# Attention start reordered: two pulls on two queues, score pairs one step later, post-mix weights loaded first

## The chip, the cores and the metric

The kernel runs on one core of one Trainium2 chip. The metric is the time of one launch on the device in microseconds (us). The engines named below are PE (TensorE, matmuls), ACT (ScalarE), DVE (VectorE), POOL (GpSimd) and SP, which computes nothing here and issues DMAs; ACT can issue DMAs too.

## The reference

Attention over 2 batches, 12 heads, 448 rows and head size 64, in which the heads are mixed by a 12x12 matrix before the softmax and by another one after it, and then two gated layers on 896 tokens of width 768 with a hidden width of 2048.

```python
scores = scale * np.matmul(q, k.transpose(0, 1, 3, 2))
scores = np.einsum('bhij,hg->bgij', scores, w_pre)
scores = scores - np.max(scores, axis=-1, keepdims=True)
attn = np.exp(scores)
attn = attn / (np.sum(attn, axis=-1, keepdims=True) + 1e-09)
attn = np.einsum('bhij,hg->bgij', attn, w_post)
out = np.matmul(attn, v)
...
h = x @ w_in
g = h * np.clip(h + 3.0, 0.0, 6.0) / 6.0
x = g @ w_out
...
h = x @ w_in
g = np.maximum(h, 0.0) + alpha * np.minimum(h, 0.0)
out = g @ w_out
```

## The kernel before

The attention rows are cut into 8 tiles, four for each batch: three of 120 rows and one of 88. A tile has 12 heads, and its scores are made as 6 pairs of heads (`qk`, L205: 8 matmul records on PE for a pair). The two score arrays of a pair lie in PSUM until they are copied to the tile's array `S` in SBUF: one by ACT, the other by DVE. The pairs take turns in two PSUM tags: in the prelude `mx` and `sc` alternate, and from step 0 on only `sc` is used, which has two buffers, room for one pair.

The mix over heads needs heads and rows on the partitions together. So `S` is rearranged by SBUF-to-SBUF DMAs, the pulls (`pull`, L221): each brings one group of up to 10 rows times 12 heads, 120 partitions, into one half of a `pull` buffer. There are 90 groups and four buffers of two groups.

The program then goes through steps p = -2 to 45 in an order written out by hand (the loop over `p_`); there is no other scheduler, and each engine runs its own instructions in that order. Step p works on groups 2p and 2p+1:

- pulls for step p+3 are issued by SP (all six for steps 0 to 2 in step -2), then the loads of v, k and q listed for this step (`load_at`, `load_q_at`);
- `premix` (L234) mixes the two groups into two PSUM buffers of tag `mx`; where a score pair is due at this step, its matmuls are emitted in between (`emit`), ACT copies one of its arrays ahead of the exponentials and DVE the other behind its maxima;
- DVE takes the row maxima (L242), ACT the exponentials (`exp`, L251), DVE the reciprocal of the sum, and POOL scales the post-mix weights `wpost` by it (`wr`, L263);
- `post` (L274) does the post-mix of step p-1, ACT copies it to `MT` (L289; one half goes to DVE once the score pairs are over), and `av` (L341, L320) multiplies finished tiles by v on some steps.

The table `qk_at` says at which step each pair of tiles 1 to 7 is made. Before the change, tile 1's six pairs stand at steps -2 and -1, three each, and the pairs of tiles 2 to 7 at steps 0 to 35, one each. Tile 0's pairs come ahead of everything. `load_q_at` follows from this table: the q of a tile is loaded 3 steps ahead of its first pair, 6 for tile 4. The k of the second batch comes in six loads, at steps 7 to 12. The first weights of the gated layers are loaded inside the same loop (`load_w`, L399, `wst`): the first block in two halves at steps 17 and 18, and ACT takes its magnitude (`conv_abs`, L411) at step 19, ahead of the post-mix copies of that step.

From about 163 us to the end the span holds the gated layers, one long chain of matmuls on PE (L529), which the change doesn't touch.

## Time and profile before

| what | value |
|---|---|
| median of the runs | 645.3 us (641.83, 645.3, 645.5) |
| profiled execution | 640.25 us, its span 638.5 us |
| PE busy | 627.0 us of the span, 98% |
| ACT, DVE, POOL busy | 345.3, 415.9, 294.0 us |
| granted TensorE clock | 0.999 of full |
| DMA | 81.69 MB, mean 128 GB/s |

The profiled execution is one run of the program, timed from outside at 640.25 us; its span, from the first to the last instruction, is what the rows show. Busy shares are means over stages that have different limits, so the stages are looked at one by one. A matmul record's end is modelled, so that a PE which waits between the parts of a mix can look busy; how far the steps lie apart shows such waits.

### The profile page before, as it was taken

The page shows a single profiled execution, that of the slowest core. Times are in us where ns is not written, and L with a number is a line of the kernel's source. Part 1 is how long each engine was busy: PE and PEld are TensorE (multiplying, and loading weights), DVE is VectorE, ACT ScalarE, POOL GpSimd, SP SyncE. Part 2 cuts the span into 40 slices and gives each one's busy share as a digit, 9 for nine tenths or more (in the row PEclk, how much of TensorE's full clock was granted, in tenths as well). Part 3 has the DMA queues.
Part 4 walks back from the last instruction along what each step waited for, and adds up shares of the span by engine and source line. Part 5 has one row for each costly group of instructions (what it writes and reads, how often), then busy time and mean ns, then how long its engine had stood idle before and what let it go on. Part 6 is the DMA issues. An engine that isn't in the chain of part 4 may idle for free.

```text
span 638.5 us, 15698 instructions
## 1 busy us (share of the span) xinstructions
PE 627.0 (98%) x6528; PEld 537.2 (84%) x6528; DVE 415.9 (65%) x653; ACT 345.3 (54%) x632; POOL 294.0 (46%) x241
## 2 busy tenths in 40 slices
PE   7999999999999999999999999999999999999997
PEld 3466667666799999999999999999999999999997
DVE  3765677778666878787545533599999996544301
ACT  4886888987645566655345433444444444444301
POOL 2221123324615454556774645355555556776430
PEclk9999999999999999999999999999999999999999
DMA  7677765756012323333442333123333333445202
GB/s 187 222 197 211 207 188 204 214 177 174 34 50 100 99 100 107 125 115 101 148 148 100 112 136 100 51 100 99 100 102 110 113 113 108 149 159 180 94 1 86
DMA packets 42163, 81.69 MB, mean 128 GB/s; under 512 B 19308, under 2 KB 32364, under 8 KB 42092
## 3 DMA queue, kind: packets, MB, share of 16 engines
q1 hardware_dynamic: 41516, 80.27, 39.5%
q8 instruction: 51, 0.84, 0.5%
q10 hardware_dynamic: 576, 0.41, 0.3%
q14 instruction: 20, 0.16, 0.1%
HBM read 58.65 MB, written 2.75 MB: 96 GB/s over the span
## 4 chain that ended last, share of the span: by engine, by line
PE 86%; POOL 4%; issue 4%; DMA 3%; DVE 1%; ACT 1%; POOLq 0%; SPq 0%; ACTq 0%
PE p L529 64%; PE sc L205 6%; PE pt L274 5%; PE mx L234 5%; PE av L341 4%; POOL wb L442 2%; POOL wlo L455 2%; DMA wst<-in_w_in_dram 2%; PE av L320 1%; DMA pull<-S 1%; ACT e L251 0%; DMA qst<-in_q_dram 0%; ACT wb L411 0%; DVE wb L427 0%; DVE wb L428 0%
## 5 line engine op out<-in xcount | busy, mean ns | idle before, releaser
L455 POOL TENSOR_TENSOR wlo<-wb,whi 128x768 fp32r<-128x768 f32 (+1 forms) x67 | 128.5, 1918 | 122.4 <-ACT whi L447 122.4
L442 POOL TENSOR_TENSOR wb<-wb,wst 128x768 int32<-128x768 int32 x64 | 125.6, 1963 | 81.7 <-DVE wb L435 67.5
L529 PE MATMUL p<-xh,whi 128*128 128x448 f32 x384 | 140.0, 364 | 0.0
L529 PE MATMUL p<-xl,whi 128*128 128x448 f32 x384 | 139.4, 363 | 0.0
L529 PE MATMUL p<-gl,whi 128*128 128x448 f32 x384 | 139.3, 363 | 0.0
L529 PE MATMUL p<-gh,wlo 128*128 128x448 f32 x384 | 138.9, 362 | 0.2 <-POOL wlo L455 0.2
L529 PE MATMUL p<-gh,whi 128*128 128x448 f32 x384 | 138.8, 361 | 0.0
L529 PE MATMUL p<-xh,wlo 128*128 128x448 f32 x384 | 138.3, 360 | 0.0
L427 DVE TENSOR_SCALAR wb<-wb 128x768 f32<-128x768 f32 x64 | 52.6, 822 | 83.4 <-ACT wb L411 83.4
L411 ACT ACTIVATE wb<-wst 128x768 f32<-128x768 f32 x64 | 58.0, 906 | 72.9 <-DMA wst<-in_w_out_dram 51.8
L447 ACT CAST whi<-wb 128x768 fp32r<-128x768 f32 x64 | 53.4, 834 | 47.7 <-PE p L529 29.5
L529 PEld LDWEIGHTS p<-xh,whi 128*128 128x128 f32 x384 | 72.1, 188 | 8.0 <-issue 1.6
L205 PE MATMUL sc<-kst,qst 64*64 64x448 f32 (+2 forms) x384 | 74.7, 575 | 3.7 <-DMA qst<-in_q_dram 3.7
L234 PE MATMUL mx<-pull,wpre 64*64 64x448 f32 (+2 forms) x360 | 74.6, 544 | 2.6 <-ACT e L251 1.7
L529 PEld LDWEIGHTS p<-gh,whi 128*128 128x128 f32 x384 | 72.0, 187 | 5.2
L529 PEld LDWEIGHTS p<-gh,wlo 128*128 128x128 f32 x384 | 71.9, 187 | 5.1 <-POOL wlo L455 0.6
L529 PEld LDWEIGHTS p<-gl,whi 128*128 128x128 f32 x384 | 72.1, 188 | 4.8
L529 PEld LDWEIGHTS p<-xh,wlo 128*128 128x128 f32 x384 | 71.8, 187 | 5.0
L529 PEld LDWEIGHTS p<-xl,whi 128*128 128x128 f32 x384 | 72.1, 188 | 3.9
L242 DVE TENSOR_REDUCE nm<-mx 128x1 f32<-128x448 f32 x90 | 55.1, 622 | 20.2 <-PE sc L205 8.9
L435 DVE SCALAR_TENSOR_TENSOR wb<-wst,wb 128x768 uint32<-128x768 uint32 x64 | 67.5, 1054 | 1.1
L263 POOL TENSOR_SCALAR wr<-wpost,sm 128x60 f32<-128x60 f32 x74 | 24.4, 345 | 93.8 <-DVE sm L259 46.6
(55 smaller groups left out, 772.7 us busy)
## 6 DMA issues: line engine op xcount, KB each, us to landing
wst<-in_w_out_dram SPq DMA_DIRECT2D x32, 768.0 KB
wst<-in_w_in_dram SPq DMA_DIRECT2D x27, 768.0 KB
pull<-S SPq DMA_DIRECT2D x88, 210.0 KB
wst<-in_w_in_dram SPq DMA_DIRECT2D x10, 384.0 KB
out_dram<-o SPq DMA_DIRECT2D x12, 224.0 KB
kst<-in_k_dram SPq DMA_DIRECT2D x11, 224.0 KB
qst<-in_q_dram SPq DMA_DIRECT2D x10, 180.0 KB
v<-in_v_dram SPq DMA_DIRECT2D x4, 168.0 KB
```

Source lines behind the costliest of these rows:

```text
L205: nc.tensor.matmul(ps[o][r:r + z - a, :S], t[D * o:D * o + D, a:z], k_[D * o:D * o + D, j, :], start=True, stop=True,)
L234: nc.tensor.matmul(ms[r][Q * c:Q * c + Q, :S], wpre[a:z], d[a:z, c, :], start=True, stop=True)
L242: nc.vector.tensor_reduce(nm, m[:, :S], axis=AX.X, op=ALU.max, negate=True)
L274: nc.tensor.matmul(ts[c][Q * z:Q * z + Q, u:u + GH], e[a:a + GH, j:j + Q], wr[a:a + GH], start=True, stop=True,)
L341: nc.tensor.matmul(by_half(p[D * o:D * o + D, a % 3, :2 * m]), v_part(T["b"], h, t), MT[ti][:, t:2 * NJ:NJ, h, :m].rearrange("p r (o x) -> ...
L411: nc.scalar.activation(t, s[:, :, 1].bitcast(F32), ACTF.Abs)
L427: nc.vector.tensor_scalar(t, t, W_MAX, W_MIN, ALU.min, ALU.max)
L435: nc.vector.scalar_tensor_tensor(u, st_t[i][:, :, 1], 0xC0000000, u, ALU.bitwise_and, ALU.bitwise_or)
L442: nc.gpsimd.tensor_tensor(n, n, st_t.pop(i)[:, :, 0].bitcast(I32), ALU.add)
L447: nc.scalar.copy(hi, b_t[i])
L455: nc.gpsimd.tensor_tensor(lo[:, a], b_t[i][:, a], w_t[i][0].bitcast(F32)[:, a], ALU.subtract)
L529: nc.tensor.matmul(p, wt[a], xt[c], start=(first and z == 0), stop=(last and z == 2))
```

## The change

Four things are changed. The second pull (group 1) is issued by ACT instead of SP. The loads of the post-mix weights (`wraw`), which stood between the fourth and the fifth pull, go ahead of all pulls, and with them the POOL copy into `wpost`. Of tile 1's six pairs, two each stay at steps -2 and -1, and the last two go to step 0, behind its mix, which is now emitted without a pair in between. All pairs of tiles 2 to 7 come one step later, at steps 1 to 36, and with them the q loads of tiles 3 to 7; the six k loads go to steps 8 to 13.

```diff
--- before.py
+++ after.py
@@ -360,7 +360,7 @@
         qk_at, av_at, av_first = {}, {}, {}
         marked = {NTILE - 1}
         for i in range((NTILE - 1) * (H // 2)):
-            p_ = i // 3 - 2 if i < H // 2 else i - H // 2
+            p_ = i // 2 - 2 if i < 4 else max(i - 5, 0)
             qk_at.setdefault(p_, []).append((1 + i // (H // 2), i % (H // 2)))
         for ti in range(NTILE - 1):
             lo = (tiles[ti]["s"] + tiles[ti]["ng"] - 1) // 2 + 2
@@ -611,6 +611,9 @@
             a = GH * c
             nc.sync.dma_start(out=wpre[Z + GH * c:Z + GH * c + GH, :GH], in_=w_pre[a:a + GH, a:a + GH])
         list(load_q(2))
+        for c in range(2):
+            a = GH * c
+            nc.sync.dma_start(out=wraw[Q * c:Q * c + GH], in_=w_post[a:a + GH, a:a + GH])
         for _ in range(4):
             d_buf.append(late.tile([128, 2, S], F32, tag=f"pull{len(d_buf)}", bufs=1, name="pull"))
             nc.gpsimd.memset(d_buf[-1][:Z], 0.0)
@@ -619,6 +622,9 @@
             v_c.append(late.tile(shape, F32, tag=f"v{c}", bufs=1, name=f"v{c}"))
         seen = late.tile([128, 16], F32, tag="rest", bufs=1, name="rest")[:, :1]
         nc.gpsimd.tensor_scalar(wpre, wpre, scale, 1.0, ALU.mult, ALU.mult)
+        nc.gpsimd.tensor_copy(
+            wpost.rearrange("p (g x) -> p x g", g=H), wraw.rearrange("p (x g) -> p x g", g=H)
+        )
 
         def s_out(pairs):
             for o, (d, s_) in enumerate(pairs):
@@ -673,24 +679,14 @@
                 load_at.setdefault(s_, []).append(lambda b=b, x=x: load_v(b, *x))
 
         for c in range(H // 2):
-            load_at.setdefault(7 + c, []).append(
+            load_at.setdefault(8 + c, []).append(
                 lambda c=c: load_k(1, c % 2, c // 2 * 2, c // 2 * 2 + 2)
             )
 
         for p_ in range(-2, NP + 1):
             if p_ == -2:
                 for g in range(6):
-                    if g == 4:
-                        for c in range(2):
-                            a = GH * c
-                            nc.sync.dma_start(
-                                out=wraw[Q * c:Q * c + GH], in_=w_post[a:a + GH, a:a + GH]
-                            )
-                        nc.gpsimd.tensor_copy(
-                            wpost.rearrange("p (g x) -> p x g", g=H),
-                            wraw.rearrange("p (x g) -> p x g", g=H),
-                        )
-                    pull(g)
+                    pull(g, nc.scalar if g == 1 else nc.sync)
             late_pull = None
             if 0 <= p_ < NP - 3:
                 g = 2 * p_ + 6
@@ -706,7 +702,7 @@
             jobs = qk_at.get(p_, [])
             pair_ = None
             if 0 <= p_ < NP:
-                if jobs:
+                if jobs and p_:
                     emit, pair_ = qk_parts(*jobs[0], "sc")
                     premix(p_, emit)
                     nc.scalar.copy(*pair_[1])
```

On PE, at the first two mixes (the numbers are the program's own count of tiles, and differ between the two programs), this stands before: tile 1's last pair, the mix of step 0 with tile 2's first pair (`qst_121`) in it, and the start of the mix of step 1.

```order
L205 MATMUL sc_234<-kst_91,qst_115 64x448
L205 MATMUL sc_234<-kst_91,qst_115 60x448
L205 MATMUL sc_235<-kst_91,qst_115 64x448
L205 MATMUL sc_235<-kst_91,qst_115 60x448
L234 MATMUL mx_251<-pull_125,wpre_95 64x448 x2
L205 MATMUL sc_250<-kst_91,qst_121 64x448
L205 MATMUL sc_250<-kst_91,qst_121 60x448
L234 MATMUL mx_252<-pull_125,wpre_95 64x448 x2
L205 MATMUL sc_249<-kst_91,qst_121 64x448
L205 MATMUL sc_249<-kst_91,qst_121 60x448
L234 MATMUL mx_282<-pull_127,wpre_95 64x448 x2
```

And now, from the mix of step 0 to the start of the mix of step 1:

```order
L234 MATMUL mx_232<-pull_127,wpre_95 64x448 x2
L234 MATMUL mx_233<-pull_127,wpre_95 64x448 x2
L205 MATMUL sc_247<-kst_91,qst_115 64x448
L205 MATMUL sc_247<-kst_91,qst_115 60x448
L205 MATMUL sc_248<-kst_91,qst_115 64x448
L205 MATMUL sc_248<-kst_91,qst_115 60x448
L205 MATMUL sc_255<-kst_91,qst_115 64x448
L205 MATMUL sc_255<-kst_91,qst_115 60x448
L205 MATMUL sc_256<-kst_91,qst_115 64x448
L205 MATMUL sc_256<-kst_91,qst_115 60x448
L234 MATMUL mx_274<-pull_129,wpre_95 64x448 x2
```

Tile 1's last two pairs (`qst_115`) have moved from ahead of the first mix to between the first and the second.

On ACT, from the copies of tile 1's last pairs (`S_197`) to the exponentials of step 1, before:

```order
L625 COPY S_197<-sc_228 124x448
L625 COPY S_197<-sc_234 124x448
L712 COPY S_248<-sc_250 124x448
L251 ACTIVATE e_267,sm_266<-mx_251,nm_261 128x448
L251 ACTIVATE e_269,sm_266<-mx_252,nm_263 128x448
L712 COPY S_248<-sc_281 124x448
L251 ACTIVATE e_298,sm_297<-mx_282,nm_292 128x448
```

And now, from the last copy of tile 0 (`S_142`) on:

```order
L631 COPY S_142<-sc_183 124x448
L221 DMA pull_127<-S_142 120x1x448
L631 COPY S_197<-sc_198 124x448
L631 COPY S_197<-sc_204 124x448
L631 COPY S_197<-sc_214 124x448
L631 COPY S_197<-sc_220 124x448
L251 ACTIVATE e_243,sm_242<-mx_232,nm_238 128x448
L251 ACTIVATE e_245,sm_242<-mx_233,nm_240 128x448
L631 COPY S_197<-sc_247 124x448
L631 COPY S_197<-sc_255 124x448
L708 COPY S_271<-sc_273 124x448
L251 ACTIVATE e_290,sm_289<-mx_274,nm_284 128x448
```

A DMA issue now stands ahead of tile 1's copies, and the copies of the two moved pairs stand behind the exponentials of step 0.

On SP, around steps 5 to 8, before (`v1` is a part of v, `qst` the q of tile 4, `kst` the k of the second batch; the pulls behind the q load are those for step 10):

```order
L221 DMA pull_127<-S_197 120x1x448 x2
L177 DMA v1_134<-in_v_dram 96x6x64
L177 DMA v1_134<-in_v_dram 32x6x64
L177 DMA v1_134<-in_v_dram 80x6x64
L177 DMA v1_134<-in_v_dram 48x6x64
L156 DMA qst_614<-in_q_dram 64x720 x2
L221 DMA pull_129<-S_197 120x1x448 x2
L119 DMA kst_92<-in_k_dram 64x896
L221 DMA pull_131<-S_197 120x1x448 x2
```

And now:

```order
L221 DMA pull_129<-S_197 120x1x448 x2
L177 DMA v1_136<-in_v_dram 96x6x64
L177 DMA v1_136<-in_v_dram 32x6x64
L177 DMA v1_136<-in_v_dram 80x6x64
L177 DMA v1_136<-in_v_dram 48x6x64
L221 DMA pull_131<-S_197 120x1x448 x2
L156 DMA qst_670<-in_q_dram 64x720 x2
L221 DMA pull_133<-S_197 120x1x448 x2
L119 DMA kst_92<-in_k_dram 64x896
```

The q load has moved behind the pulls for step 10, and the first k load behind those for step 11.

## Rows read from the trace of the kernel before

**Rows 1.** The page: busy time, and PE in 40 equal slices of the span.

```profile
PE 627.0 (98%) x6528; PEld 537.2 (84%) x6528; DVE 415.9 (65%) x653; ACT 345.3 (54%) x632; POOL 294.0 (46%) x241
...
PE   7999999999999999999999999999999999999997
```

**Rows 2.** Busy time by stretch: length, each engine's busy time and instructions, clock, DMA.

```profile
16.30:21.30 5.00, 4.46 (x42) 1.29 (x36) 3.72 (x8) 3.00 (x8) 0.70 (x3) 1.00 0.54 200
...
37.00:61.00 24.00, 22.67 (x554) 15.30 (x550) 13.46 (x32) 17.25 (x43) 4.50 (x14) 1.00 0.74 204
61.00:81.00 20.00, 20.00 (x557) 13.73 (x556) 13.34 (x32) 16.19 (x42) 3.49 (x13) 1.00 0.71 208
...
163.00:638.50 475.50, 471.67 (x2661) 438.85 (x2660) 303.93 (x385) 218.27 (x320) 249.60 (x133) 1.00 0.31 104
```

**Rows 3.** PE's matmuls in order of time, steps 0 and 1: start, length, what.

```profile
16.34 0.59 PE L234 MATMUL mx<-pull,wpre 64*64 64x448 f32 x2
...
19.34 0.59 PE L234 MATMUL mx<-pull,wpre 64*64 64x448 f32 x2 [0.51 <-ACT e L251]
...
21.27 1.08 PE L274 MATMUL pt<-wr,e 60*64 60x60 f32 x55
```

**Rows 4.** SP's DMA issues in order of time.

```profile
8.84 1.27 SPq L161 DMA_DIRECT2D qst<-in_q_dram  x2
12.56 3.42 SPq L221 DMA_DIRECT2D pull<-S  x4
16.03 1.19 SPq L686 DMA_DIRECT2D wraw<-in_w_post_dram  x2
17.26 8.46 SPq L221 DMA_DIRECT2D pull<-S  x10
...
41.83 1.19 SPq L156 DMA_DIRECT2D qst<-in_q_dram  x2
43.11 1.78 SPq L221 DMA_DIRECT2D pull<-S  x2
```

**Rows 5.** The chain that ended last: start, length, what.

```profile
43.11 4.75 DMA pull<-S
...
77.24 6.57 DMA wst<-in_w_in_dram
...
138.38 0.76 PE mx L234 x8
```

**Rows 6.** PE's matmuls at the mix of step 10.

```profile
47.99 1.52 PE L234 MATMUL mx<-pull,wpre 64*64 64x448 f32 x3 [0.81 <-DMA pull<-S]
```

**Rows 7.** ACT: the first exponentials of steps 9, 11, 13 and 15.

```profile
44.43 0.64 ACT L251 ACTIVATE e<-mx,nm 128x448 f32<-128x448 f32 x1
...
53.86 0.64 ACT L251 ACTIVATE e<-mx,nm 128x448 f32<-128x448 f32 x1
...
61.01 0.64 ACT L251 ACTIVATE e<-mx,nm 128x448 f32<-128x448 f32 x1
...
67.88 0.66 ACT L251 ACTIVATE e<-mx,nm 128x448 f32<-128x448 f32 x1
```

**Rows 8.** DVE in order of time: the last copy of tile 0, and two maxima.

```profile
11.88 0.62 DVE L625 COPY S<-sc 124x448 f32<-124x448 f32 x1 [0.32 <-PE sc L205]
...
23.14 1.38 DVE L242 TENSOR_REDUCE nm<-mx 128x1 f32<-128x448 f32 x2
```

**Rows 9.** ACT's sequencer at the start: a DMA issue of 128 partitions.

```profile
0.74 0.39 ACTq L115 DMA_DIRECT2D kst<-in_k_dram  x1
```

**Rows 10.** ACT in order of time, 12 to 23 us.

```profile
12.51 0.53 ACT L625 COPY S<-sc 124x448 f32<-124x448 f32 x1 [0.25 <-PE sc L205]
...
19.09 0.20 ACT L251 ACTIVATION_READ_ACCUMULATOR e<-mx,nm 128x1 f32 x1
...
22.05 0.64 ACT L251 ACTIVATE e<-mx,nm 128x448 f32<-128x448 f32 x1
```

**Rows 11.** Waits from 60 to 110 us: who waited for whom, total, times, longest.

```profile
ACT wb L411 <- DMA wst<-in_w_in_dram: 1.4, 1, 1.4
```

## The prediction, made before the changed kernel ran

> **What bounds the kernel now.** The page comes first: PE is busy for 98% of the span, and its only slice under 9 tenths is the first one (and the last) [rows 1]. Then the windows: from 163 us to the end PE has 471.67 us of work in 475.50 us [rows 2], all in the gated layers. The change doesn't touch them, so the end moves only by as much as the end of attention does. Inside attention the same view tells where time can be had. The stretch 37 to 61 us takes 24.0 us for 554 matmul records, the stretch 61 to 81 us takes 20.0 us for 557 [rows 2]: they hold the same work, six steps each (7 to 12 and 13 to 18), one tile's product with v in each, and differ by 4.0 us of waits. The other place is the ramp, where the first two mixes and the first post-mix follow each other: 16.34, 19.34 and 21.27 us, with a gap of 0.51 us on PE [rows 3].
>
> Last come SP's issues and the chain of waits. SP is issuing almost without a pause from 12.56 us on: four pulls in 3.42 us, the post-mix weights in 1.19, ten pulls in 8.46 [rows 4], some 0.85 us a pull. So it falls behind, and the pulls for step 10 go out only at 43.11 us. They have landed 4.75 us later, and the chain runs through them [rows 5]. PE stands idle for 0.81 us, and the three mix records behind that take 1.52 us together [rows 6], so the wait is longer than the gap. The exponentials give its full size: from step 9 to step 11 it takes 53.86 - 44.43 = 9.43 us, from step 13 to step 15, with the same work, 67.88 - 61.01 = 6.87 us [rows 7]. That is 2.56 us of the 4.0.
>
> **The change part by part.** First **the ramp**, followed from row to row. DVE is done with tile 0 at 12.50 us [rows 8], and both queues can start to pull then. ACT now issues a pull there. Its price isn't in the trace: an issue of 128 partitions took ACT 0.39 us at the start [rows 9], SP needs 3.42 / 4 = 0.86 us for a pull [rows 4]. I take 0.86, since that is the same transfer. ACT then takes up its copies of tile 1 at 13.42 us, where it began at 12.51 [rows 10], and this reaches PE: the third pair needs the `mx` buffers of the first, whose ACT copy (0.53 us) ends at 13.95. With 0.76 us for 8 records of a pair (the eight of a lone mix in the chain took that, [rows 5]) the third pair ends at about 14.75 and the fourth at 15.5, and the first mix can begin there instead of at 16.34. The pulls are not late by then if they land as now, but only if.
>
> The gain of 0.8 us is given back at once. The mix ends at 16.25; two maxima take DVE 1.38 us [rows 8], so to 17.7; the second exponentials, 0.64 us [rows 10], end at 18.35, and only behind them, by the new order on ACT, come the copies of the two moved pairs. Tag `sc` has room for one pair, so the second moved pair waits for ACT's copy of the first: with 0.2 us to read the sums of the exponentials and 0.53 for the copy [rows 10] it starts at 19.1 and ends at 19.85. The mix of step 1 stands behind it on PE: 19.85 instead of 19.34, 0.5 us late, and PE has stood idle for some 2 us in between. Inside that mix, tile 2's first pair needs the same two buffers, copied (0.53 us on ACT, 0.62 on DVE) by about 20.5, where PE would be at 20.25: 0.3 us more. So the first post-mix comes **0.8 us later** than now, and waiting behind it are the POOL and DVE steps of the same step and all later ones. Bounds: if the second pair needn't wait, the two pairs end at 16.25 + 2 x 0.76 = 17.8 us, where the mix of step 1 can start, 1.5 us sooner than now; if ACT's pull takes the 4.75 us that the pulls at 43.11 took to land [rows 5], the first mix begins at 17.3 us instead of 15.5, and the post-mix 0.8 + 1.8 = 2.6 us late.
>
> Second, **one pair more is left**. When the first post-mix starts, PE has done one pair fewer than before: tile 2's second pair, which stood in the mix of step 1. Every step up to 35 has one pair as before, and step 36 gets one where it had none. The chain lies on PE there, with the lone mix of 8 records in it [rows 5], so I charge a pair of 8 records at **+0.76 us**; the lower bound is 0, if it fits into a wait there. The copy of half of the post-mix of step 35 moves from DVE to ACT; PE sets the pace there by the same rows, so I cost it at nothing, and at one such copy, some 0.6 us, as the upper bound.
>
> Third, **SP's queue**. Taken off it ahead of the pulls for step 10 are one pull (0.86 us), the post-mix weights (1.19 us, now in SP's pause between 8.84 + 1.27 = 10.11 and 12.56 [rows 4]; POOL's copy of them is due only at the first post-mix), and the q load of tile 4, which moves behind them (41.83 to 43.11, 1.28 us). Sum: 3.3 us, so they go out at 39.8 and, with the same 4.75 us, have landed at 44.5. PE asks for them at 47.2 now (47.99 less the gap of 0.81) and, with the ramp's loss, at 48.0. There are 3.5 us to spare, so the stall of 2.56 us goes: **-2.56 us**. Next in line behind it is the q load, then the pulls for step 11, which get 3.3 - 1.3 + 0.75 of a k load = 2.8 us sooner. Bounds: nothing, if the transfers and not their issue are late; -4.0 us, if all the waits of that stretch come from SP.
>
> At this place the Trainium skill speaks against the change. "DMA: Bandwidth & Descriptors", section "Issuing engines are not separate DMA queues", says that DMAs of all issuing engines run on the same 16 DMA engines, and that a second issuing engine saves the sequencer's time alone, usually small beside the transfer. By that rule the stall would stay and the time would be that of the third rival. The rows are against it in this stretch: ten issues fill 8.46 us [rows 4] while the DMA engines are busy for 0.54 to 0.74 of the time [rows 2], so issuing is not small here.
>
> Fourth, **the weights of the gated layers**. Their second half is issued at 77.24 us and lands 6.57 us later [rows 5]; ACT waits 1.4 us for it at step 19 [rows 11], and all of ACT's queue waits too. The q load of tile 5 and the last k load now come one step closer to it. As pulls and loads ahead of it all go out some 2 us sooner, I leave this wait as it is: 0, with -1.4 us (it goes) and +1.8 us (it eats what was won by then) as bounds. The q loads of tiles 6 and 7 still have two steps and more to land: nothing.
>
> **The sum**: 0.8 + 0.76 - 2.56 = **-1.0 us** on the profiled execution: 640.25 becomes 639.25. The median of the runs, 645.3, is 5 us above that execution; the shift is the same for it, so I predict **644.3 us**.
>
> **The rivals.** (1) *Slower: the weights' landing is fixed.* If the second half of the weights lands at 83.83 us whatever the attention does, since the same bytes go ahead of it, ACT at step 19 loses again what was won (0.8 - 2.56 = -1.76), and only the pair at step 36 is left: +0.76, 646.1. It decides as soon as that wait is over 1.4 + 1.76 = 3.2 us. For it: the landing takes 6.57 us, against 4.75 for pulls; against it: SP reaches it sooner too. (2) *The ramp wins.* The moved pairs fill PE's wait without waiting themselves: -1.5 + 0.76 - 2.56 = -3.3, 642.0. For it: the gap of 0.51 us shows that PE has room there; against: one pair of `sc` buffers, and ACT's order. (3) *Slower: the change doesn't relieve SP's stall*, as the pulls for step 10, or those for step 11 behind the moved q load, land late all the same: 0.8 + 0.76 = +1.56, 646.9. For it: k, q and pulls still share one queue; against: 3.5 us to spare.
>
> **How the numbers follow.** The forecast gets 0.45, the rivals 0.2, 0.2 and 0.15. The range takes in the rivals' times and the runs' own spread: from the lowest run less 1.0, 641.83 - 1.0 = 640.8, to the highest with the third rival, 645.5 + 1.56 = 647.1. A measurement of this kernel can tell about 1% (6.4 us) from no change, and no case here comes near that. Faster by over 1% needs the ramp's gain, all 4.0 us of waits and the weights' 1.4 us at once: 0.03. Slower by over 1% needs something that I don't see: 0.02. Slower than before at all has 0.35.
>
> **What would show it.** Right: the mix of step 1 begins later than 19.34 us, at 19.85, behind a wait of PE of about 2 us for ACT's copy; the first post-mix is at 22.1; the pulls for step 10 are issued near 39.8 us and no step from 9 to 11 takes over 4.3 us; step 36 is 0.76 us longer. Wrong: a mix of step 1 ahead of 19 us (rival 2), an ACT wait of 3 us for the weights at step 19 (rival 1), a pull in the chain near 48 us (rival 3), or a stall at a step past 19 that isn't there now.

## The result, and the profile after

The changed kernel takes 647.88 us (median of 22 runs, 643.79 to 652.09) beside 644.27 for the kernel before (22 runs). The medians differ by 3.6 us; the ratio on record, which is not that of the medians, is 1.0073, with a 95% interval of 1.0048 to 1.0098: **4.7 us slower** (3.1 to 6.3), where 1.0 us faster was forecast. The median lies outside the forecast range, whose upper end was 647.1. The profiled execution took 646.29 us with a span of 644.5, 6.0 us longer than before. Slower at all had a chance of 0.35, within 1% of before 0.95; both came.

The loss lies in attention, as foreseen: the first exponentials of step 44 start at 173.14 us instead of 167.00, so the gated layers add nothing. First the start. In order of time, ACT from the last copy of tile 0 to the exponentials of step 1 answers to [rows 10]:

```profile
12.74 1.68 ACTq L221 DMA_DIRECT2D pull<-S  x1
14.46 0.97 ACT L631 COPY S<-sc 124x448 f32<-124x448 f32 x2 [1.95 <-PE sc L205]
...
18.37 0.64 ACT L251 ACTIVATE e<-mx,nm 128x448 f32<-128x448 f32 x1 [1.02 <-DVE nm L242]
...
19.61 0.53 ACT L631 COPY S<-sc 124x448 f32<-124x448 f32 x1
21.20 0.53 ACT L631 COPY S<-sc 124x448 f32<-124x448 f32 x1 [1.07 <-PE sc L205]
...
23.23 0.64 ACT L251 ACTIVATE e<-mx,nm 128x448 f32<-128x448 f32 x1
```

PE in the same stretch answers to [rows 3]:

```profile
15.05 1.73 PE L205 MATMUL sc<-kst,qst 64*64 64x448 f32 x16 [0.75 <-ACT S L631]
16.70 1.10 PE L234 MATMUL mx<-pull,wpre 64*64 64x448 f32 x8
17.47 1.08 PE L205 MATMUL sc<-kst,qst 64*64 64x448 f32 x8
20.19 0.98 PE L205 MATMUL sc<-kst,qst 64*64 64x448 f32 x8 [1.64 <-ACT S L631]
20.99 0.92 PE L234 MATMUL mx<-pull,wpre 64*64 64x448 f32 x4
...
22.74 0.43 PE L274 MATMUL pt<-wr,e 60*64 60x60 f32 x6
...
23.35 0.85 PE L274 MATMUL pt<-wr,e 60*64 60x60 f32 x42
```

The first mix is not sooner than before (16.70 against 16.34), because ACT is held for 1.68 us by its pull and PE waits 0.75 us for the copies behind it. Then the wait that was foreseen is there: 1.64 us on PE for ACT's copy of the first moved pair (19.61 to 20.14). The exponentials of step 1 start at 23.23 instead of 21.25.

SP's issues, in order of time, answer to [rows 4]:

```profile
12.73 15.42 SPq L221 DMA_DIRECT2D pull<-S  x13
28.20 1.85 SPq L177 DMA_DIRECT2D v<-in_v_dram  x3
...
31.88 2.84 SPq L177 DMA_DIRECT2D v<-in_v_dram  x4
34.83 1.35 SPq L161 DMA_DIRECT2D qst<-in_q_dram  x2
...
44.76 1.69 SPq L221 DMA_DIRECT2D pull<-S  x2
46.54 1.19 SPq L156 DMA_DIRECT2D qst<-in_q_dram  x2
```

With two pulls' worth of work less ahead of it, SP is not earlier but later: 13 pulls take 15.42 us, 1.19 us each where ten took 8.46. There are four pull buffers of two groups, and a pull into one that is in use waits until PE has read it. After nine pulls SP stands still from 20.60 to 23.54 us, since the mixes of steps 0 and 1 are late. Of SP's waits from 12 to 29 us the largest group is

```profile
SPq L221 <- PE pt L274: 4.7, 2, 3.3
```

The pulls for step 10 go out at 44.76 us, not at 39.8. And the q load of tile 3, in the third row from the end above, goes out at 34.83 us, behind four more loads of v. In the kernel before it went out at 27.75:

```profile
27.75 1.31 SPq L161 DMA_DIRECT2D qst<-in_q_dram  x2
```

The first exponentials of the steps 8, 9, 11, 13, 15, 19 and 20 (the first four after step 8 answer to [rows 7]):

```profile
44.60 0.64 ACT L251 ACTIVATE e<-mx,nm 128x448 f32<-128x448 f32 x1
...
47.20 0.65 ACT L251 ACTIVATE e<-mx,nm 128x448 f32<-128x448 f32 x1
...
53.98 0.63 ACT L251 ACTIVATE e<-mx,nm 128x448 f32<-128x448 f32 x1
...
60.48 0.66 ACT L251 ACTIVATE e<-mx,nm 128x448 f32<-128x448 f32 x1
...
67.44 0.66 ACT L251 ACTIVATE e<-mx,nm 128x448 f32<-128x448 f32 x1
...
84.67 0.67 ACT L251 ACTIVATE e<-mx,nm 128x448 f32<-128x448 f32 x1
...
88.96 0.64 ACT L251 ACTIVATE e<-mx,nm 128x448 f32<-128x448 f32 x1
```

Step 9 to 11 takes 6.78 us instead of 9.43: the stall is gone, as forecast. (Here and below, "step n takes" is the time from the exponentials of step n-1 to those of step n.) Taken over all steps, the same exponentials in both traces say where the time went:

| from step to step | before, us | after, us | difference |
|---|---|---|---|
| start to 8 | 41.09 | 44.60 | +3.51 |
| 8 to 15 | 26.79 | 22.84 | -3.95 |
| 15 to 19 | 13.18 | 17.23 | +4.05 |
| 19 to 20 | 5.52 | 4.28 | -1.24 |
| 20 to 32 | 39.21 | 41.31 | +2.10 |
| 32 to 37 | 16.72 | 18.29 | +1.57 |
| 37 to 44 | 24.50 | 24.58 | +0.08 |

After step 15 the changed kernel is 0.44 us ahead, and it then loses 6.6 us. Part of this is waits of PE, two of them between 69 and 78 us:

```profile
70.76 0.97 PE L274 MATMUL pt<-wr,e 60*64 60x60 f32 x50 [1.31 <-issue]
...
76.46 1.10 PE L205 MATMUL sc<-kst,qst 64*64 64x448 f32 x8 [1.46 <-DMA qst<-in_q_dram]
```

The view puts the first down to nothing ("issue") and the second to a q load, which would be tile 5's. But the pair made there, at step 17, is one of tile 4 and needs no row of tile 5 (one semaphore tells of this load and of a k load that the pair does need). A third wait, of 1.18 us, comes at step 27. All three, 3.95 us together, are waits for PE's own instructions, as is shown further down.

The wait for the weights at step 19 [rows 11] is gone, but the same kind of wait, for the third block of them, has grown at step 34. Before, in the waits of 118 to 150 us:

```profile
ACT wb L411 <- DMA wst<-in_w_in_dram: 0.9, 1, 0.9
```

And now:

```profile
ACT wb L411 <- DMA wst<-in_w_in_dram: 1.7, 1, 1.7
...
PE pt L274 <- ACT MT L289: 0.6, 1, 0.6
```

### The profile page after: what moved, and what is told of

Same layout as the page of the kernel before. It is cut to its first block, busy times and chain, and to the rows that moved or that the text cites. A ratio compares the mean times of both kernels' runs of the same rounds, so it can differ in the third digit from the quotient of the medians.

```text
span 644.5 us, 15691 instructions
## 1 busy us (share of the span) xinstructions
PE 627.7 (97%) x6528; PEld 538.3 (84%) x6528; DVE 417.5 (65%) x652; ACT 345.7 (54%) x633; POOL 293.0 (45%) x241
## 4 chain that ended last, share of the span: by engine, by line
PE 86%; POOL 4%; issue 4%; DMA 3%; DVE 1%; ACT 1%; ACTq 0%; SPq 0%; POOLq 0%
PE p L529 64%; PE pt L274 6%; PE mx L234 5%; PE sc L205 5%; PE av L341 5%; POOL wb L442 2%; POOL wlo L455 2%; DMA qst<-in_q_dram 1%; PE av L320 1%; DMA kst<-in_k_dram 1%; DMA wst<-in_w_in_dram 1%; ACT e L251 0%; DVE nm L242 0%; ACTq L221 0%; ACT wb L411 0%
## 5 line engine op out<-in xcount | busy, mean ns | idle before, releaser
L455 POOL TENSOR_TENSOR wlo<-wb,whi 128x768 fp32r<-128x768 f32 (+1 forms) x67 | 126.9, 1895 | 122.0 <-ACT whi L447 122.0
L205 PE MATMUL sc<-kst,qst 64*64 64x448 f32 (+2 forms) x384 | 72.9, 561 | 8.2 <-DMA qst<-in_q_dram 5.2
L234 PE MATMUL mx<-pull,wpre 64*64 64x448 f32 (+2 forms) x360 | 73.2, 543 | 1.0 <-ACT e L251 0.5
L435 DVE SCALAR_TENSOR_TENSOR wb<-wst,wb 128x768 uint32<-128x768 uint32 x64 | 70.8, 1107 | 1.1
```

Of the source, the lines that this page charges most:

```text
L205: nc.tensor.matmul(ps[o][r:r + z - a, :S], t[D * o:D * o + D, a:z], k_[D * o:D * o + D, j, :], start=True, stop=True,)
L234: nc.tensor.matmul(ms[r][Q * c:Q * c + Q, :S], wpre[a:z], d[a:z, c, :], start=True, stop=True)
L435: nc.vector.scalar_tensor_tensor(u, st_t[i][:, :, 1], 0xC0000000, u, ALU.bitwise_and, ALU.bitwise_or)
L455: nc.gpsimd.tensor_tensor(lo[:, a], b_t[i][:, a], w_t[i][0].bitcast(F32)[:, a], ALU.subtract)
```

## The experiments

All ratios are to the kernel before, run beside it. The runs fall into groups on four chips, so ratios of different groups compare less well. Theory A put the loss on the moved pairs and what moves with them, rival B on the pull that ACT issues; after the first four runs A became A', with its parts named, and rival C took the later waits for chance. A 95% interval here is about 0.0033 either way, some 2 us, so single runs tell less than groups of them.

| run | ratio | interval | runs with a mean granted clock of 0.9985 or more |
|---|---|---|---|
| changed kernel | 1.0073 | 1.0048 to 1.0098 | 5 of 22 |
| `p1_after_again` | 1.0060 | 1.0020 to 1.0101 | 2 of 12 |
| `p2_queue_weights` | 1.0014 | 0.9978 to 1.0051 | 4 of 12 |
| `p3_pairs_only` | 1.0097 | 1.0062 to 1.0131 | 1 of 11 |
| `p4_one_queue` | 1.0096 | 1.0068 to 1.0124 | 0 of 11 |
| `r5_q3_early` | 1.0044 | 1.0009 to 1.0079 | 4 of 12 |
| `r6_second_pair_pt` | 1.0027 | 0.9994 to 1.0060 | 3 of 12 |
| `r7_one_pair` | 1.0110 | 1.0078 to 1.0143 | 2 of 12 |
| `r8_shift_only` | 1.0072 | 1.0038 to 1.0106 | 4 of 12 |
| `r9_q3_and_pt` | 1.0027 | 0.9995 to 1.0058 | 6 of 12 |
| `r10_all_q_and_pt` | 1.0017 | 0.9985 to 1.0049 | 8 of 12 |
| `r11_q4_later` | 1.0007 | 0.9975 to 1.0040 | 3 of 12 |
| `r12_third_weights` | 0.9959 | 0.9933 to 0.9985 | 12 of 12 |
| `r13_before_third` | 0.9988 | 0.9962 to 1.0015 | 9 of 12 |
| `r14_after_third` | 1.0034 | 1.0002 to 1.0067 | 5 of 12 |
| `r15_old_pairs_best` | 1.0000 | 0.9970 to 1.0030 | 8 of 12 |
| `r16_third_and_q3` | 1.0011 | 0.9990 to 1.0033 | 9 of 12 |
| `r17_best_one_queue` | 0.9972 | 0.9939 to 1.0004 | 9 of 12 |
| `r18_old_pairs_one_queue` | 0.9981 | 0.9952 to 1.0010 | 10 of 12 |

One fall to half for 3.4 us, as in the profile of `p3_pairs_only`, takes 0.0026 off a run's mean clock, so the last column counts the runs without one. The kernel before had 39 to 63% of its runs at that clock, by group.

### Which part of the change loses

**The changed kernel once more**, no edit. 

> The changed kernel once more, for a second profile. Theory A (the loss has three parts: the ramp, 2.0 us at the exponentials of step 1; the pair at step 36, 0.7 us; and waits at steps 16, 17, 27, 32 and 34 that follow from the loads' new places and eat the stall of steps 9 to 13 that went): about 4 us slower than before, and the waits of 1.3 to 1.5 us at steps 16 and 17 come again. Rival B (the waits past step 13 are chance; the loss is the ACT-issued pull alone): as slow, with those waits gone or elsewhere in this profile.

649.61 us, 1.006: as slow. Of the waits of PE that theory A named, those of steps 17 and 27 came again and that of step 16 didn't. The profiled execution took 651.36 us, 5.07 more than the first one of the same kernel, and this difference is the lesson: at step 7 PE waits for tile 3's q, until 0.1 us after the last part of it has landed, and from 39.37 to 46.19 us the granted clock is at half. Busy time by stretch (columns as in [rows 2]; the third number from the end is the granted clock):

```profile
34.00:39.00 5.00, 3.83 (x98) 2.10 (x90) 3.49 (x10) 4.38 (x13) 1.20 (x5) 1.00 0.74 184
39.00:46.00 7.00, 5.74 (x36) 3.19 (x36) 1.49 (x4) 1.88 (x5) 0.91 (x2) 0.53 0.73 206
46.00:60.00 14.00, 14.00 (x410) 9.81 (x410) 8.67 (x20) 10.75 (x28) 2.42 (x8) 0.99 0.76 231
```

PE there, in order of time:

```profile
40.26 1.86 PE L205 MATMUL sc<-kst,qst 64*64 64x448 f32 x8 [2.44 <-DMA qst<-in_q_dram]
...
43.41 2.67 PE L341 MATMUL av<-MT,v 128*64 128x120 f32 x24
```

The 24 records of `av` take 2.67 us, 1.38 at full clock in the chain of the kernel before. Steps 7 and 8 take 6.47 and 6.55 us, against 3.33 and 4.54 in the first profile of this kernel: 5.15 us, about as much as the two executions differ by.

**Only the second queue and the weights**: pairs, q and k loads as before. 

> The changed kernel with all score pairs and k loads where they were: only the second pull on ACT and the post-mix weights ahead. Theory A: ACT is held by its pull issue for some 1.7 us, so step 1 comes about 0.9 us late, but SP is 2 us ahead and step 10 waits less: between -1.5 and +0.5 us. Rival B: the ACT-issued pull is the loss: +2 to +4 us.

644.72 us, 1.0014, or 0.9 us (-1.4 to 3.3): no difference that can be told, and between what theory A and rival B expected. The first exponentials start at 20.21 us in its profile, 1.65 later than before, since all six pairs of tile 1 now stand behind ACT's pull.

**Only the pairs**, with their q and k loads; no second queue, weights where they were. 

> The kernel before with only the pairs, their q loads and the k loads moved; SP issues both first pulls and the weights' loads stay behind the fourth pull. Theory A: the second moved pair waits for ACT as in the changed kernel, step 1 is 1.2 to 1.5 us late, step 36 0.7 us longer: +2 to +4 us. Rival B: no loss without the ACT-issued pull: within 1 us of before.

650.01 us, 1.0097, or 6.2 us: more than the 2 to 4 that theory A expected. The moved pairs carry the loss by themselves. PE waits 1.65 us at the start and 1.47 for tile 3's q at 39.40 us, and the granted clock is 0.63 in the 4.6 us behind that.

**All but the second queue.**

```diff
-                    pull(g, nc.scalar if g == 1 else nc.sync)
+                    pull(g)
```

> The changed kernel with the second pull back on SP. Theory A: ACT starts on tile 1 about 1.7 us sooner, step 1 is some 0.7 us sooner than in the changed kernel, so +3 to +4 us against before. Rival B: the loss goes: within 1 us of before.

649.76 us, 1.0096, no better without ACT's pull, and again more than theory A expected. Rival B fell. Theory A's own 0.7 us at step 1 didn't come either: PE now waits for the pulls at the first mix, and the first exponentials are no sooner.

```profile
16.16 1.39 PE L234 MATMUL mx<-pull,wpre 64*64 64x448 f32 x5 [0.43 <-DMA pull<-S]
```

```profile
18.52 0.64 ACT L251 ACTIVATE e<-mx,nm 128x448 f32<-128x448 f32 x1 [2.55 <-DVE nm L242]
```

### Which wait of the moved pairs loses

**Tile 3's q back at step 3.**

```diff
-  load_q_at.setdefault(p_ - (6 if ti == tps else 3), []).append(ti)
+  load_q_at.setdefault(p_ - (6 if ti == tps else 4 if ti == 3 else 3), []).append(ti)
```

> The changed kernel, with the q rows of tile 3 loaded four steps ahead of its first pair (at step 3, where they were loaded before), not three (at step 4, behind four more loads of v). Theory A' (the loss has several parts: some 2 us at the start, where the second pair behind the first mix waits for ACT; 0.7 us at step 36; and the q load of tile 3, which now lands after the pair that needs it, at step 7, for a wait of 0.7 to 2.4 us and a granted clock that falls to half for some microseconds behind it in most executions): the wait at step 7 and the half clock behind it go, and the kernel is 1 to 3.5 us over the kernel before, ratio 1.002 to 1.0055. Rival C (the loss is the start and step 36 alone; the waits for q and the clock come and go with the execution and don't carry): 4 to 5.5 us over before, ratio 1.006 to 1.0085, as the changed kernel.

646.21 us, 1.0044, inside what A' expected. The profile shows the mechanism undone: step 7 takes 2.62 us, step 8 4.26, with the clock at 1.00 from 36 to 46 us. The time went elsewhere in part: PE waited 1.94 us at step 15 (for instructions, see below) and 1.88 us at 138.01, for ACT, and behind the latter the clock was at half for 3 us.

**The second moved pair in the free post-mix banks.**

```diff
-            two = [lambda ti=ti, j=j: qk(ti, j, "mx" if p_ < 0 and j % 2 == 0 else "sc") for ti, j in jobs]
+            two = [lambda ti=ti, j=j: qk(ti, j, "mx" if p_ < 0 and j % 2 == 0 else "pt" if p_ == 0 and j == 5 else "sc") for ti, j in jobs]
```

> The changed kernel, with the second of the two moved pairs (the last pair of tile 1) written to the two banks of post-mix results, which are free until step 1, in place of the two banks of scores that wait for ACT to empty the first moved pair. If the start is a main part of the loss (theory A', 2 us at the exponentials of step 1, most of it this wait of 1.64 us on TensorE): these exponentials come 1 to 1.7 us sooner than in the changed kernel and the kernel is 2.5 to 4 us over before, ratio 1.004 to 1.006. If the later waits (the q load at step 7, the clock behind it, steps 17 and 27) are what counts and set the time again however early the start is: as the changed kernel, 4 to 6 us over before, ratio 1.006 to 1.0095.

645.55 us, 1.0027, better than either expectation. ACT copies both pairs in one go, and the exponentials of step 1 start at 21.55 us, 1.68 sooner than in the changed kernel:

```profile
19.52 0.96 ACT L631 COPY S<-sc 124x448 f32<-124x448 f32 x2
21.12 0.53 ACT L708 COPY S<-sc 124x448 f32<-124x448 f32 x1 [0.64 <-PE sc L205]
21.55 0.64 ACT L251 ACTIVATE e<-mx,nm 128x448 f32<-128x448 f32 x1
```

Step 7's wait for q stays, 2.39 us here.

**One pair behind the first mix, not two.**

```diff
-  p_ = i // 2 - 2 if i < 4 else max(i - 5, 0)
+  p_ = i // 3 - 2 if i < 5 else i - 5
```

> The changed kernel with one pair of tile 1 behind the first mix, not two (three at step -2, two at step -1, one at step 0); tiles 2 to 7 one step later, as changed. Theory A': no second pair waits for ACT, so the exponentials of step 1 come about 0.5 us later than before and not 2 us later; with the q load of tile 3 still late, 2.5 to 4.5 us over before, ratio 1.004 to 1.007. If the start is all of the loss: 0 to 2 us over before, ratio 1.000 to 1.003. If the shift of tiles 2 to 7 is all of it: as the changed kernel, 1.006 to 1.0095.

649.25 us, 1.011: a miss. The second pair's wait is gone, but five pairs stand ahead of the first mix behind ACT's pull and its exponentials start at 20.20 us, so those of step 1 are at 23.46, as late as in the changed kernel; PE waits 2.02 us for tile 3's q, and the granted clock is at half for 7 us behind it.

**Tile 1's pairs as before, tiles 2 to 7 one step later.**

```diff
-  p_ = i // 2 - 2 if i < 4 else max(i - 5, 0)
+  p_ = i // 3 - 2 if i < H // 2 else i - 5
```

> The changed kernel with the six pairs of tile 1 three and three ahead of the first mix, as before; only tiles 2 to 7 are one step later, with their q and k loads, and the second pull stays on ACT and the post-mix weights ahead of the pulls. Theory A': the start is as before (exponentials of step 1 within 0.5 us of before), the wait at step 7 for the q rows of tile 3 is there and the pair at step 36 too, 1.5 to 4 us over before, ratio 1.002 to 1.006. If the start is all of the loss: 0 to 1 us over before. If the shift is all of it: as the changed kernel, 4 to 6 us over.

646.64 us, 1.0072 (1.0038 to 1.0106): the full loss, as far as the interval tells, with the exponentials of step 1 only 0.57 us late. Theory A' expected less; the shift with its loads is enough for the loss. PE waits 1.81 us for tile 3's q, and then, at step 34, 4.59 us for ACT, which waits 5.9 us for the third block's weights. PE, in order of time, and the stretch behind both waits:

```profile
140.73 2.17 PE L274 MATMUL pt<-wr,e 60*64 60x60 f32 x56 [4.59 <-ACT MT L289]
```

```profile
39.00:43.00 4.00, 4.00 (x34) 2.30 (x26) 1.28 (x3) 1.88 (x5) 0.00 (x0) 0.57 0.74 201
...
138.00:145.00 7.00, 4.27 (x71) 2.71 (x72) 3.52 (x8) 4.81 (x11) 0.60 (x2) 0.51 0.37 135
```

### The waits together

**Tile 3's q early and the post-mix banks**, both edits. 

> The changed kernel with both edits at once: tile 3's q loaded four steps ahead of its first pair, and the second moved pair in the banks of post-mix results. If these two waits are parts of the loss that add up (theory A'): neither the gap of 1.64 us ahead of mix 1 nor the wait at step 7 nor the half clock behind it is there, and the kernel is 0 to 1.5 us over the kernel before, ratio 1.000 to 1.0025. If an early start is given back at a later wait, whatever it is (rival): no better than with one of the two, 1.6 to 3 us over, ratio 1.0025 to 1.0045.

645.04 us, 1.0027, at the rival's end: not better than the banks alone. In its profile neither wait is there and the clock stays at full, but step 27 takes 3.67 us (2.54 before) and steps 16 and 17 together 10.23, against 6.76 before: the waits for instructions again.

**The q of tiles 5 to 7 back too**, so that only tile 4's is later than before. 

> The kernel of the run with both edits, and the q rows of tiles 5, 6 and 7 loaded four steps ahead of their first pair too, so that all q loads but tile 4's stand at the steps where they stood before. If these loads, one step nearer to the loads of weights and to the pairs that need them, cause the waits at step 17 (1.5 us in two profiles) and for the third block's weights at steps 32 to 34 (1.2 to 2.3 us on ACT more than before): 0.5 to 1.5 us less than that run, ratio to before 0.998 to 1.001. If those waits come from where the loads fall among the pulls in one execution: the same as that run within 0.001, and ACT still waits 2 to 3 us for the third block's weights.

643.34 us, 1.0017, within what the comparison can tell of the run above. Step 17 takes 2.59 us here, but 4.43 in the next run, which loads q at the same steps, so these loads don't decide the wait there. ACT still waits 3.6 us for the third block's weights and PE 2.28 behind it: that wait doesn't hang on these loads either.

**The third block of weights converted two steps later**, on top of that kernel; its loads stay.

```diff
-            odd = (a + 2) | 1
+            odd = (a + 2 + 2 * (i == 2)) | 1
```

> The kernel with all q loads but tile 4's as before and the second moved pair in the banks of post-mix results; the third block of weights is converted two steps later (its absolute value on ACT at step 35, not 33), with its loads where they were, so that ACT need not wait for their landing. If the wait of ACT for these weights (1.7 to 3.2 us in the profiles of the moved pairs, 0.9 before) is a part of the loss: 0.5 to 2 us less than the same kernel without this edit, steps 32 to 34 take 1 to 2 us less. If the wait only takes the place of another (the pulls or the copies of that stretch): the same within 0.001.

641.44 us, **0.9959 (0.9933 to 0.9985)**: faster than both kernels (643.28 us is the median of the kernel before beside it, 1.8 us more, so by the medians the gain is less). ACT has no wait for weights from 118 to 150 us, step 34 takes 4.19 us (6.01 in the changed kernel, 5.16 before), and all 12 runs were at full clock. At full clock it takes no less than the kernel before: 641.5 us on the mean of its runs, 641.3 on that of the 17 runs of the kernel before that were at this clock. What it gains over the kernel before is that the clock no longer falls.

**The same edit on the kernel before.** 

> The kernel before, with one edit: the third block of weights is converted two steps later, its loads where they were. If the wait for these weights is in the kernel before as well (0.9 us on ACT in its profile, and a granted clock below 0.9985 in more than half of its executions): 0.5 to 2.5 us less than before, ratio 0.996 to 0.999, and more of its executions at full clock. If the wait is a part of what the change brought: within 0.5 us of before, ratio 0.9985 to 1.0015, and the clock as before.

641.76 us, 0.9988 (0.9962 to 1.0015): step 34 takes 4.23 us, but the time can't be told from before. It lies in the overlap of both expectations; that wait is in the kernel before too, only smaller.

**The same edit alone on the changed kernel.** 

> The changed kernel, with the third block of weights converted two steps later and nothing else. Theory A': the wait at step 34 and the half clock behind it go, the wait at step 7 for tile 3's q and the start's loss stay: 1 to 2.5 us less than the changed kernel, 2.2 to 4 us over before, ratio 1.0035 to 1.006. If the waits of step 34 take time only beside the others: as the changed kernel, 1.006 to 1.0095.

645.23 us, 1.0034: 0.0039 under the changed kernel, as A' expected or a little more, though not past the noise of the two.

**Third weights and tile 3's q** on the changed kernel, the start unmended. 

> The changed kernel, with the third block of weights converted two steps later and tile 3's q loaded four steps ahead of its first pair; the second moved pair still waits for ACT. Theory A': neither of the two waits behind which the clock fell is left, so the clock stays at full in nearly all executions and what is left of the loss is the start (some 1.7 us) against a kernel before whose clock falls in half of its executions: 0 to 1.5 us over before, ratio 1.000 to 1.0025. If the wait of 1.64 us at the start brings the clock down as well, or the clock falls whatever the waits are: 2 to 4 us over before, ratio 1.003 to 1.006.

643.47 us, 1.0011, as A' expected, 9 of 12 runs at full clock. The wait of 1.64 us at the start doesn't bring the clock down.

### The other sides

**Tile 4's q behind the pulls of step 10**, in the kernel before.

```diff
-  load_q_at.setdefault(p_ - (6 if ti == tps else 3), []).append(ti)
+  load_q_at.setdefault(p_ - (5 if ti == tps else 3), []).append(ti)
```

> The kernel before, with one edit: the q rows of tile 4 are loaded five steps ahead of its first pair, not six, that is behind the pulls of step 10 and not ahead of them. Theory A' takes the stall of step 10 (6.2 us, 4.2 in the changed kernel) for the one real gain of the change, and it hangs on this load's wait on SP alone: step 10 takes about 4.2 us, some 1 to 2.6 us less in all, ratio 0.996 to 0.9985. If the wait for the weights at step 19 (1.4 us on ACT) gives it back: 0 to 1 us less, ratio 0.9985 to 1.0.

645.28 us, 1.0007: a miss. Step 10 takes 5.23 us instead of 6.21, step 11 4.08 instead of 3.22; from step 9 to 11 that is 9.31 against 9.43. The stall isn't this load's alone.

**The old order of pairs with the other edits** (second pull on ACT, weights ahead, tile 4's q later, third block later). 

> Pairs, q and k loads as in the kernel before; the second pull on ACT and the post-mix weights ahead of the pulls as changed; tile 4's q five steps ahead of its first pair (not six); the third block of weights converted two steps later. If the moved pairs bring nothing of their own, this is as fast as the best so far or faster: 2 to 4.5 us under before, ratio 0.993 to 0.997. If the moved pairs are worth something once their waits are gone: 0 to 2 us under before, ratio 0.997 to 1.000.

642.61 us, 1.0000. Its first exponentials start at 20.85 us, 2.3 later than before, PE having waited 1.34 us behind ACT's pull. The expectation takes this for a sign that the moved pairs are worth something; the next two runs, without ACT's pull, don't bear it out.

**Both orders, mended, on one queue.** 

> The kernel with the new order of pairs and its three waits mended (tile 3's and the later q rows but tile 4's loaded as early as before, the second moved pair in the banks of post-mix results, the third block of weights converted two steps later), with the second pull back on SP. If the new order is worth something once mended and the queue of the second pull nothing: 1 to 4 us under before, ratio 0.994 to 0.9985, and full clock in nearly all executions. If the second queue carried it: 0.9985 to 1.002.

> The old order of pairs with the weights of the post-mix ahead of the pulls, tile 4's q five steps ahead of its first pair, the third block of weights converted two steps later, and all pulls on SP. If the order of pairs is worth nothing either way: as the mended new order in the same batch, within 0.0015. If the mended new order is the better one: 0.002 to 0.004 above it, ratio to before 0.997 to 1.001. Against the same kernel with its second pull on ACT (1.0): the same if the queue is worth nothing.

642.06 us, 0.9972, and 642.77, 0.9981: the same. Once its waits are mended the new order of pairs is worth nothing over the old one that can be measured, and no gain of the second queue shows (0.9959 with it, 0.9972 without, in different groups).

## Why the prediction was wrong

**What failed.** Three terms were wrong: the q loads, put at nothing; the gain at the start of the ramp; and the third block of weights, which was not in the sum. The largest term, SP's queue, came out right by luck. First the q loads. The sentence "The q loads of tiles 6 and 7 still have two steps and more to land: nothing" passes over tile 3's. The q loads follow the pairs, three steps ahead; for tile 3 that means from step 3 to step 4, behind four loads of v. With the late start its issue moves by 7.1 us (27.75 to 34.83), while PE comes only 2.4 us later (the exponentials of step 6 at 36.73, 34.30 before). The wait at step 7 is there with the pairs alone, without the second queue, and with the start as before; with the load back at step 3 step 7 takes 2.6 to 2.9 us in all six profiles. Its price is 0.7 us in the first profile and 2.4 in the second, and the granted clock that falls to half behind it makes that 5.15.

**The ramp** was mis-sized: +0.8 us forecast at the first post-mix, +1.5 to +2.1 measured (its first six records at 22.74, the others from 23.35, against 21.27), +2.0 at the exponentials of step 1. The wait for ACT's copy came as foreseen (some 2 us forecast, 1.64 measured). The term that failed is the gain ahead of it: ACT's pull was priced at 0.86 us like one of SP's and took 1.68, and the first mix was 0.36 us later, not 0.8 sooner. Without ACT's pull the pulls themselves are late (`p4_one_queue`), so the condition that the prediction set, "The pulls are not late by then if they land as now", fails as well. The second rival, that the ramp wins, fell: the mix of step 1 begins at 20.99 us, not ahead of 19.

**SP's queue** gave the forecast gain by luck. The pulls for step 10 were to go out at 39.8 us and went out at 44.76, later than before, because SP doesn't issue freely: the pulls wait for their buffers, and so for the mixes that the ramp delays. The stall went all the same (-2.65 us from step 9 to 11, -2.56 forecast), but it goes only behind the wait of step 7. In the eight profiles of the moved pairs with tile 3's q at step 4, step 9 to 11 takes 6.76 to 6.78 us. In the six with that load back at step 3 it takes 8.60 (`r5_q3_early`), 7.80 (`r9_q3_and_pt`), 8.84 (`r10_all_q_and_pt`), 6.86 (`r12_third_weights`), 8.26 (`r16_third_and_q3`) and 9.01 (`r17_best_one_queue`). So the work taken off SP is not what removed the stall; PE had lost the time already, at the start and at step 7, and by the exponentials of step 11 the changed kernel stands at 53.98 us against 53.86. The third rival, that the stall stays, didn't come in this kernel, but in three of the six profiles (`r5`, `r10`, `r17`) PE waits 0.97 to 1.37 us at step 11 for a pull, as that rival had it. The run with tile 4's q load alone moved shows that this load isn't the whole cause of the stall; what else is, stays open.

**The pair at step 36** cost 0.68 us (3.29 against 2.61 up to step 37's exponentials), 0.76 forecast.

**The weights.** The wait at step 19 that the first rival lived from went away (1.24 us won); the same wait for the third block, at step 34, was not in the working, though the trace of before had 0.9 us of it; "a stall at a step past 19 that isn't there now" was one of the prediction's own signs of being wrong. It grew to between 1.4 and 5.9 us in the profiles of the moved pairs with the third block where it was, though also to 3.1 us in the one with the old pairs and the second queue. Together with tile 3's q and the start it makes the loss: pairs of kernels that differ by one edit give 0.0046 and 0.0017 for the post-mix banks, 0.0029, 0.0023 and 0 for tile 3's q, 0.0039, 0.0033 and 0.0058 for the third block. Two of these are past the noise of two such ratios, some 0.0041: 0.0046, which compares two groups, and 0.0058, where the medians of the one group differ by less (643.34 and 641.44 us, 0.0030). The other six are not. The three together, with the q of tiles 5 to 7, are well past it: 1.0073 (from 1.0048 up) becomes 0.9959 (to 0.9985) and, on one queue, 0.9972 (to 1.0004). Nor is the loss all clock: the runs at full clock have a mean of 645.5 us for the changed kernel (5 runs), 642.5 for `r10_all_q_and_pt` (8), 641.5 for `r12_third_weights` (12) and 641.3 for the kernel before beside these two (17).

**The second queue.** At this start the rows now agree with the rule of the Trainium skill that the prediction weighed ("DMA: Bandwidth & Descriptors", "Issuing engines are not separate DMA queues"): a second issuing engine adds no DMA engines. The DMA queues of the changed kernel in the stretches 14.0 to 15.2, 15.2 to 16.0 and 16.0 to 17.0 us (q1 is SP's, q10 ACT's; packets, MB, share of 16 engines), one answer each:

```profile
q1 hardware_dynamic: 127, 0.22, 46.8%
```

```profile
q10 hardware_dynamic: 112, 0.20, 64.8%
```

```profile
q1 hardware_dynamic: 148, 0.25, 64.4%
```

The packets of SP's first pull, of ACT's and of SP's second follow one another instead of running side by side. Whether the rule also decides the stall of step 10, as the rival had it, no run settles.

**The waits that the view puts down to nothing.** They come at steps 14 to 17 and 27 in most kernels here, the mended ones too, and the trace does tell their cause. PE's instructions come in packets of 16 KB on the queue q8, one for every 256 records of PE (51 packets for 13,209 records in the changed kernel). From 68 to 70 us, just ahead of the wait at 70.76:

```profile
q8 instruction: 1, 0.02, 3.3%
```

In the 20 profiles together, PE has 32 such waits of over 0.55 us between 20 and 163 us. Counted from PE's first record, every one stands ahead of a record whose number leaves 193 or 194 when it is divided by 256, and every one ends 1.3 to 1.7 us after a q8 packet has ended. So PE waits there for its next 256 instructions. Five more stand at the same places (remainder 194 or 195) though the view names a releaser, among them the wait of step 17 in both profiles of the changed kernel; in the second one PE went on at 79.31 us, before the q load that is named had landed in full (80.10). These waits add up to 3.95 us in the first profile of the changed kernel, 2.79 in the second, 3.06 in that of `r12_third_weights` and there is none of that length in that of the kernel before. So they are a good part of the 6.0 us between the first two profiles, but not what makes `r12_third_weights` the faster kernel.

**What stays open.** Whether the change makes PE's waits for instructions longer or more frequent isn't shown: no edit was aimed at them, and they differ between two executions of one kernel. Nor is it shown why the changed order with one pair behind the first mix is slower than with two, or why the shift alone, with the start nearly as before, loses as much as the whole change.

## What to carry to other kernels

When a table that places work is moved by one step, list every load whose place is derived from it, with its issue, its landing and the first reader in the trace, not only the loads whose waits show today; here one with no wait before brought a wait of up to 2.44 us. Before a stall that has gone is booked as a gain, see that the time wasn't lost ahead of it; here it had been. Moving work out of a stretch with waits of its own (two pairs of the prelude, behind the pulls) brought nothing that could be measured. A small wait of TensorE can cost twice its length through the granted clock (2.44 us of wait, 5.15 in all), so look for the clock in several executions before a wait of 2 us is priced at 2 us. And where a view puts a wait down to nothing, or to a load that the instruction doesn't need, compare its place in the program and the packets of the instruction queue.

## What the runs showed of the hardware

The granted clock fell to half (1.2 of 2.4 GHz) for 3 to 7 us in the middle of attention, each time in or behind a wait of PE: 1.47 to 2.44 us at step 7 in all six profiles where the wait for tile 3's q was that long, 1.82 to 4.59 us at step 34 in five, 1.83 at step 14 (`p2_queue_weights`) and 1.62 at step 17 (`p1_after_again`). It didn't after waits of 0.35 to 1.16 us at step 34, nor after 1.64 at the start, 1.79 to 1.94 at step 15 in three profiles, 1.46 at step 17, or 2.06 at step 13 (`p2_queue_weights`), so the length of the wait alone doesn't decide. Two executions of the same kernel differed by 5.07 us, and the two steps around one such fall by 5.15.

A pull issued by ACT while SP issued its own held ACT for 1.40 to 1.75 us in the 13 profiles that have it, where SP needed 0.93 to 0.95 for its first one.

PE's instructions are loaded in 16 KB packets, 256 records each, and PE stood still for up to 2.06 us where one came late: all 32 waits of over 0.55 us without a releaser stand at such a place.
